# Banded attention and a token/channel mixer on one core: the next batch's attention interleaved with this batch's channel layer, scores by key chunk, gathers once

## The chip, the cores and the metric

The kernel runs on one core of a Trainium2 chip. The metric is the device time of one execution in microseconds (us); lower is better. The core has five engines that run side by side, each with its own queue in order: TensorE (PE, matmuls; its weight loads are listed as PEld), VectorE (DVE), ScalarE (ACT), GpSimd (POOL) and SyncE (SP, which here only issues DMAs). Matmul results land in PSUM (8 banks of 512 float32 columns on 128 partitions) and are read from there by DVE or ACT.

## The reference

```python
scores = scale * np.matmul(q, k.transpose(0, 1, 3, 2))     # q, k, v: (8, 8, 576, 64)
mask = np.abs(pos[:, None] - pos[None, :]) <= 32
mask = mask | is_global[:, None] | is_global[None, :]      # 8 global positions
attn = softmax(np.where(mask, scores, -1e9))
x = (attn @ v), heads side by side                         # (8, 576, 512)
h = np.maximum(x.T @ w_tok1, 0.0) @ w_tok2                 # 576 -> 256 -> 576, per channel
u = x + h.T
out = u + np.maximum(u @ w_ch1, 0.0) @ w_ch2               # 512 -> 1536 -> 512
```

Eight batches are computed one by one. The 576 positions make four tiles of 128 and a leftover of 64.

## The kernel before

One loop over the batches `b`; the code of a batch is written attention first, then the two mixer layers. A framework allots buffers from pools, sets the waits and orders each engine's queue; a later batch can run ahead only as far as that order and the buffers allow.

Attention, per head pair `hp`: ten transposes bring q and k to `qT`, `kT` (L244, copied out of PSUM by DVE at L250, L252). Four small matmuls (L258, L259) transpose the global rows, which eight one-row DMAs per tensor and batch have gathered (L223). Per head then: for each of five shifted key chunks `c` two or three score matmuls (L274, L277, L284) whose weights are the 64x128 half of `kT` that belongs to the head, `Exp` on ACT (L287), the band mask on DVE (L288); two matmuls of the global keys against all queries (L291, L292); five `og` matmuls for the global queries (L298); and for each query tile up to four matmuls of 65 columns (L310, L312, L313, L314), a reciprocal and a product on DVE (L316, L317) into `x16`.

Mixer: `pa1` (L326) and `ph_` (L339) are the token layer, `pu` (L352) transposes `u16` to `uT`. `pb1` (L362) is the first channel matrix: 24 groups of four matmuls of 288 columns, `Relu` on ACT (L369). `ph2` (L374) is the second: five groups of twelve matmuls of 512 columns, the last with 64 query rows only, then the addition of `u16` on DVE (L382) and the store, issued by ACT (L383).

Ahead of the loop stand masks, and the four weight matrices: loaded as float32 by SP and cast to float16 by ACT (L161 to L177). The first is loaded ahead of batch 0's q.

Of the kernel before, what the change touches and what calls it, by code (L numbers as in the profile page):

```python
# [9 lines left out]
F32 = mybir.dt.float32  # L11
F16 = mybir.dt.float16
I32 = mybir.dt.int32
AF = mybir.ActivationFunctionType
ALU = mybir.AluOpType


@with_exitstack
def kernel(
# [36 lines left out]
    nat = ctx.enter_context(tc.tile_pool(name="nat", bufs=3))
    ab = ctx.enter_context(tc.tile_pool(name="ab", bufs=2))
    hb = ctx.enter_context(tc.tile_pool(name="hb", bufs=2))
    pb = ctx.enter_context(tc.tile_pool(name="pb", bufs=3))
    mb = ctx.enter_context(tc.tile_pool(name="mb", bufs=2))  # L60
    ob = ctx.enter_context(tc.tile_pool(name="ob", bufs=2))
    tiny = ctx.enter_context(tc.tile_pool(name="tiny", bufs=3))
    psA = ctx.enter_context(tc.tile_pool(name="psA", bufs=5, space=bass.MemoryType.PSUM))
    psM = ctx.enter_context(tc.tile_pool(name="psM", bufs=3, space=bass.MemoryType.PSUM))

    def psa(shape, dtype=F32, name="pa"):
        return psA.tile(shape, dtype, tag="a", name=name)

    def psm(shape, dtype=F32, name="pm"):
# [17 lines left out]
    iota_i_i = const.tile([P, S], I32)
    nc.gpsimd.iota(iota_i_i, pattern=[[1, S]], base=0, channel_multiplier=0)
    iota_if = const.tile([P, S], F32)
    nc.vector.tensor_copy(out=iota_if, in_=iota_i_i)  # L90
    iota_p_i = const.tile([P, 1], I32)
    nc.gpsimd.iota(iota_p_i, pattern=[[1, 1]], base=0, channel_multiplier=1)
    iota_pf = const.tile([P, 1], F32)
    nc.vector.tensor_copy(out=iota_pf, in_=iota_p_i)

    colng = const.tile([P, S], F16)
    tmp_s = const.tile([P, S], F32, tag="set576")
    nc.vector.tensor_scalar(out=colng, in0=iota_if, scalar1=gidx_bf[:, 0:1], scalar2=None, op0=ALU.not_equal)
    for g in range(1, NG):
        nc.vector.tensor_scalar(out=tmp_s, in0=iota_if, scalar1=gidx_bf[:, g : g + 1], scalar2=None, op0=ALU.not_equal)  # L100
        nc.vector.tensor_mul(out=colng, in0=colng, in1=tmp_s)

    iota_tm_i = const.tile([P, NT, P], I32)
    nc.gpsimd.iota(iota_tm_i, pattern=[[P, NT], [1, P]], base=0, channel_multiplier=0)
    iota_tmf = const.tile([P, NT, P], F32)
    nc.vector.tensor_copy(out=iota_tmf, in_=iota_tm_i)
    selq = const.tile([P, NT, P], F16)
    nc.vector.tensor_scalar(
        out=selq[0:NG], in0=iota_tmf[0:NG], scalar1=gidx_pf[0:NG, 0:1], scalar2=None, op0=ALU.is_equal
    )  # L110
# [303 lines left out]
```

## Time and profile before

| | us |
|---|---|
| median of the timed runs | 717.95 (712.82, 717.95, 717.98) |
| profiled execution, first to last instruction | 716.0 |
| its PE busy / DVE / ACT / POOL | 613.9 / 315.9 / 298.4 / 6.4 |
| first `Exp` of batch 0 | 76.8 |
| from one batch's attention to the next's | about 80 |

The profile holds no time of its execution other than that span; the median of the timed runs lies 1.95 us above it. A matmul's row runs until its result has left the array, so rows of a stream overlap: the cost of one in a stream is the distance from start to start, not its duration. The granted clock is a share of TensorE's full speed.

### The profile page before, as it was taken

How to read it: one execution, taken by the hardware profiler on the slowest of the kernel's cores; microseconds unless marked ns; L12 is line 12 of the kernel's file. 1: busy time of each engine (PE TensorE's matmuls, PEld its weight loads, DVE VectorE, ACT ScalarE, POOL GpSimd, SP SyncE). 2: the span in 40 equal slices, each digit the busy share in tenths (PEclk: the TensorE clock that was granted, in tenths of full speed). 3: DMA queues.
4: the chain of work that ended last, by engine and by line, in shares of the span. 5: the costliest groups of instructions: out<-in, count | busy, mean ns of one | idle time of the engine just before them, and what ended most of it. 6: DMA issues, size and time to landing. Idle time of an engine off the chain costs nothing.

```text
span 716.0 us, 12722 instructions
## 1 busy us (share of the span) xinstructions
PE 613.9 (86%) x4576; PEld 366.7 (51%) x4576; DVE 315.9 (44%) x1441; ACT 298.4 (42%) x742; POOL 6.4 (1%) x27
## 2 busy tenths in 40 slices
PE   0001599999999999999999999999999999999997
PEld 0000365555646566555546565656556555656563
DVE  2800355326552456415551456326651565145521
ACT  1243364416525453346326533554337432523350
POOL 3000000000000000000000000000000000000000
PEclk9999999995559855796569855995579756975599
DMA  1992553026300907013600436020900100010001
GB/s 48 287 250 33 93 111 69 1 88 113 62 1 3 204 5 134 0 50 85 114 15 16 126 70 123 1 78 5 198 1 30 41 2 1 16 52 2 1 1 66
DMA packets 125054, 46.43 MB, mean 65 GB/s; under 512 B 117504, under 2 KB 118080, under 8 KB 124992
## 3 DMA queue, kind: packets, MB, share of 16 engines
q1 hardware_dynamic: 119744, 36.19, 25.5%
q10 hardware_dynamic: 5248, 9.44, 3.8%
q8 instruction: 35, 0.57, 0.4%
q14 instruction: 27, 0.22, 0.1%
HBM read 36.18 MB, written 9.44 MB: 64 GB/s over the span
## 4 chain that ended last, share of the span: by engine, by line
PE 74%; DVE 8%; DMA 6%; SPq 6%; ACT 3%; issue 2%; ACTq 0%; DVEq 0%
SPq L223 2%; DMA w_32_216<-in_moe_w_tok_dram 2%; DMA wc_32_226<-in_moe_w_ch_dram 2%; SPq L200 1%; SPq L192 1%; SPq L182 1%; ACT wc_228 L172 1%; DMA w_32_222<-in_moe_w_tok_dram 1%; DMA n_1_2_2532<-in_k_dram 1%; DMA out_dram<-osb_3_1373 0%; PE ph_5_0_6982 L374 0%; PE ph_7_4_9314 L374 0%; PE ph_3_4_4778 L374 0%; PE ph_2_4_3644 L374 0%; PE ph_1_4_2510 L374 0%
## 5 line engine op out<-in xcount | busy, mean ns | idle before, releaser
L362 PEld LDWEIGHTS <-wc_228 128*128 128x128 f16 x768 | 75.0, 98 | 19.6
L244 PE MATMUL pT_0_0_332<-ident,qn_277 128*128 128x128 f16 (+1 forms) x5 | 0.8, 292 | 40.3 <-ACT qn_277 L208 40.3
L314 PEld LDWEIGHTS <-selq 8*128 8x128 f16 (+1 forms) x320 | 27.7, 123 | 5.3 <-issue 3.1
L244 PEld LDWEIGHTS <-qn_277 128*128 128x128 f16 (+1 forms) x20 | 1.8, 125 | 41.5 <-ACT qn_277 L208 40.3
L326 PEld LDWEIGHTS <-w_219 128*128 128x128 f16 (+1 forms) x80 | 9.1, 123 | 24.6 <-issue 24.1
L244 PE MATMUL pT_0_1_339<-ident,kn_278 128*128 128x128 f16 (+1 forms) x5 | 0.8, 293 | 15.9 <-ACT kn_278 L208 15.9
L244 PEld LDWEIGHTS <-kn_278 128*128 128x128 f16 (+1 forms) x20 | 1.8, 126 | 17.0 <-ACT kn_278 L208 16.0
L339 PEld LDWEIGHTS <-w_224 128*128 128x128 f16 (+1 forms) x80 | 7.8, 114 | 5.2 <-issue 3.3
L172 ACT CAST wc_228<-wc_32_226 128x6144 f16<-128x6144 f32 x1 | 5.3, 5312 | 10.8 <-DMA wc_32_226<-in_moe_w_ch_dram 10.8
L258 PE MATMUL pG_0_346<-ident,qg_320 8*64 8x8 f16 x2 | 0.2, 210 | 11.2 <-DVE qg_320 L227 11.2
L374 PEld LDWEIGHTS <-b_5_6837 128*128 128x128 f16 (+1 forms) x60 | 5.9, 100 | 7.4 <-issue 0.8
L374 PEld LDWEIGHTS <-b_0_1167 128*128 128x128 f16 (+1 forms) x60 | 5.9, 100 | 7.0 <-issue 0.4
L374 PEld LDWEIGHTS <-b_1_2301 128*128 128x128 f16 (+1 forms) x60 | 5.9, 100 | 7.0 <-issue 0.4
L374 PEld LDWEIGHTS <-b_4_5703 128*128 128x128 f16 (+1 forms) x60 | 5.9, 100 | 7.0 <-issue 0.4
L374 PEld LDWEIGHTS <-b_3_4569 128*128 128x128 f16 (+1 forms) x60 | 5.9, 100 | 7.0 <-issue 0.4
L374 PEld LDWEIGHTS <-b_2_3435 128*128 128x128 f16 (+1 forms) x60 | 5.9, 100 | 7.0 <-issue 0.4
L374 PEld LDWEIGHTS <-b_7_9105 128*128 128x128 f16 (+1 forms) x60 | 5.9, 100 | 7.0 <-issue 0.4
L374 PEld LDWEIGHTS <-b_6_7971 128*128 128x128 f16 (+1 forms) x60 | 5.9, 100 | 7.0 <-issue 0.4
L177 ACT CAST wc_232<-wc_32_230 128x6144 f16<-128x6144 f32 x1 | 5.3, 5311 | 9.0 <-DMA wc_32_230<-in_moe_w_ch_dram 9.0
L252 DVE COPY kT_0_329<-pT_0_1_339 128x576 f16<-128x576 f16 x1 | 0.5, 458 | 16.2 <-PE pT_0_1_339 L244 16.2
L287 ACT ACTIVATE E_0_353<-sc_0_0_354 128x136 f16<-128x136 f32 x1 | 0.3, 284 | 15.9 <-PE sc_0_3_371 L284 15.9
L382 DVE TENSOR_TENSOR osb_0_9263<-u_7_9053,ph_7_0_9250 128x512 f32<-128x512 f16 x1 | 0.7, 687 | 14.1 <-PE ph_7_0_9250 L374 14.1
(5049 smaller groups left out, 1988.4 us busy)
## 6 DMA issues: line engine op xcount, KB each, us to landing
wc_32_226<-in_moe_w_ch_dram SPq DMA_DIRECT2D x1, 3072.0 KB
wc_32_230<-in_moe_w_ch_dram SPq DMA_DIRECT2D x1, 3072.0 KB
n_0_0_258<-in_q_dram SPq DMA_DIRECT2D x4, 256.0 KB
n_1_0_264<-in_k_dram SPq DMA_DIRECT2D x4, 256.0 KB
n_0_1_1392<-in_q_dram SPq DMA_DIRECT2D x4, 256.0 KB
n_1_1_1398<-in_k_dram SPq DMA_DIRECT2D x4, 256.0 KB
n_0_2_2526<-in_q_dram SPq DMA_DIRECT2D x4, 256.0 KB
n_1_2_2532<-in_k_dram SPq DMA_DIRECT2D x4, 256.0 KB
```

The source lines that it names most:

```text
L172: nc.scalar.copy(out=wc1, in_=wc1_32)
L177: nc.scalar.copy(out=wc2, in_=wc2_32)
L182: nc.sync.load(r, gidx_i[0:1, g : g + 1])
L192: nc.sync.dma_start(out=d32[0 : np_t[t], t], in_=ten[b, :, P * t : P * t + np_t[t], :].rearrange("h p d -> p h d"),)
L200: nc.sync.dma_start(out=d32[r0:r1, t], in_=ten[b, :, j0 : j0 + (r1 - r0), :].rearrange("h p d -> p h d"),)
L223: nc.sync.dma_start(out=d32[g : g + 1], in_=ten[b, :, ds(gregs[g], 1), :].rearrange("h one d -> one h d"))
L244: nc.tensor.transpose(out=pT[:, P * t : P * t + npt], in_=src[0:npt, t, 2 * hp : 2 * hp + 2, :], identity=ident[0:npt, 0:npt],)
L314: nc.tensor.matmul(ox[0:nq], lhsT=selq[0:NG, tau, 0:nq], rhs=ogs, start=False, stop=True)
L326: nc.tensor.matmul(pa1, lhsT=w1[0:npt, ch, P * tt : P * tt + P], rhs=x16[0:npt, ch, :], start=(ch == 0), stop=(ch == NT - 1),)
L339: nc.tensor.matmul(ph_[0:nq], lhsT=w2[:, ch, P * tau : P * tau + nq], rhs=a1[:, ch, :], start=(ch == 0), stop=(ch == 1),)
L362: nc.tensor.matmul(pb1, lhsT=wc1[:, cc, P * j : P * j + P], rhs=uT[:, cc, NSH * half : NSH * half + NSH], start=(cc == 0), stop=(cc == 3),)
L374: nc.tensor.matmul(ph2[0:nq], lhsT=b1[:, j, P * tau : P * tau + nq], rhs=wc2[:, j, :], start=(j == 0), stop=(j == 11),)
```

## The change

The program is written anew as functions: `T` (transposes of a head pair), `S_` (scores of a pair), `GK`, `OG`, `PV` (attention), `M1` to `M3` (token layer and transposes), `M4`, `M5` (channel layer). `sparse(b)` lists the first eight of batch `b`, `dense(b)` the channel layer, and `merge` writes `sparse(b + 1)` and `dense(b)` into each other by the costs given with each piece.

- Scores: queries lie as `[8 global | 128]` per tile, so that one matmul per head and key chunk gives the 64 nearest columns of the tile ahead, the global columns and the tile itself (200 or 136 columns); the two heads of a pair use rows 0-63 and 64-127 and fill one PSUM tile, which ACT reads in one instruction.
- Global keys of all eight heads come from eight matmuls (`GK`), global queries of all heads from ten (`OG`); `PV` takes both corrections as one more matmul of 264 columns per half, 18 matmuls a tile (10 for the last).
- The 64 leftover rows of an even batch and of the next odd one share one 128-row tile in `M4l` and `M5`.
- Global rows are gathered once, for all batches, by 16 indirect DMAs of POOL. The weights are loaded by POOL's queue with a cast to float16. POOL also casts v, copies global columns and clears borders.
- q, k and v have one float32 buffer each; the load for `b + 2` waits for the cast of `b + 1`.
- PSUM: two 2-bank tiles for `T`, `S_`, `GK`, `OG`, `M1`, `M2`; one for `PV`, `M3`; two 1-bank tiles for `M4`, `M5`. Before: 5 and 3 single banks.

```diff
+def merge(sparse, dense):
...
+        if j >= len(dense) or (i < len(sparse) and a / ts <= d / td):
+            a += sparse[i][0]
+            sparse[i][1]()
...
+        else:
+            d += dense[j][0]
+            dense[j][1]()
...
+    for b in range(B):
+        nc.gpsimd.indirect_dma_start(
+            out=v32g[b], out_offset=None, in_=rows[2],
...
+    nc.gpsimd.dma_start(out=w1, in_=moe_w_tok1[0 : S - LAST, :].rearrange("(c p) x -> p c x", p=P))
...
+        nc.scalar.copy(out=s["qn"][:, sl], in_=n32[0][:, sl])
+        nc.vector.tensor_copy(out=s["kn"][:, sl], in_=n32[1][:, sl])
+        nc.gpsimd.tensor_copy(out=vsh[b % 2][:, sl, :, 0:D], in_=n32[2][:, sl])
...
+            for par in range(2):
+                r = slice(64 * par, 64 * par + 64)
+                nc.tensor.matmul(
+                    ps[:, par, off : off + n], lhsT=kT[r, P * c : P * c + P], rhs=qf[r, lo : lo + n],
+                    start=True, stop=True,
+                )
...
+        nc.gpsimd.tensor_copy(
+            out=eg[:, :, 2 * p : 2 * p + 2, 0:NG], in_=e2[:, :, :, P:QS].rearrange("p h c x -> p c h x")
+        )
...
+        u += [(0.6, lambda p=p: T(b, p)) for p in range(2)]
+        u += [(0.5, lambda: S_(b, 0)), (0.6, lambda: T(b, 2)), (0.5, lambda: S_(b, 1)), (0.6, lambda: T(b, 3))]
+        u += [(0.5, lambda: S_(b, 2)), (0.5, lambda: S_(b, 3)), (0.4, lambda: GK(b)), (1.1, lambda: OG(b))]
+        u += [(0.8, lambda t=t: PV(b, t)) for t in range(NT)]
...
+        u = [(0.86, lambda j=j: M4(b, j)) for j in range(NJ)]
+        if b % 2:
+            u += [(0.9, lambda j=j: M4l(b, j)) for j in range(3)]
+        u += [(0.64, lambda t=t, i=i: M5(b, t, i)) for t in range(4 + b % 2) for i in range(4)]
...
+        if b + 2 < B:
+            load(b + 2)
+        merge(sparse(b + 1) if b + 1 < B else [], dense(b))
```

TensorE's queue where batch 2's first channel matrix ends, before:

```order
L362 MATMUL pb1_2_11_0_3568<-uT_2_3404,wc1_228 128x288
L362 LDWEIGHTS wc1_228
...
L362 MATMUL pb1_2_11_1_3574<-uT_2_3404,wc1_228 128x288
L374 LDWEIGHTS b1_2_3435
L374 MATMUL ph2_2_0_3580<-wc2_232,b1_2_3435 128x512
```

And in the change, where batch 2's `M4` (`b1p`) stands with batch 3's scores (`s1`, `s2`) and transposes (`pT`):

```order
L492 MATMUL b1p_2_3_1859<-uT_2_1716,wc1_274 128x512
L336 LDWEIGHTS kT_3_1_1806
L336 MATMUL s1_3_1_1865<-qT_3_1_1805,kT_3_1_1806 128x200
...
L492 MATMUL b1p_2_4_1884<-uT_2_1716,wc1_274 128x512
L336 LDWEIGHTS kT_3_1_1806
L336 MATMUL s2_3_1_1871<-qT_3_1_1805,kT_3_1_1806 128x136
...
L315 LDWEIGHTS qn_3_1747
L315 MATMUL pT_3_3_1890<-ident_108,qn_3_1747 128x128
```

Between two groups of the channel layer now stand a group of scores or ten transposes of the next batch.

ScalarE's queue at the same place, before (`b1` is the Relu of the channel layer, `a1` that of the token layer):

```order
L295 ACTIVATE Egk_2_7_3318<-gk2_2_7_3315 8x64
L333 ACTIVATE a1_2_3368<-pa1_2_0_3369 128x512
L333 ACTIVATE a1_2_3368<-pa1_2_1_3376 128x512
L369 ACTIVATE b1_2_3435<-pb1_2_0_0_3436 128x288
L369 ACTIVATE b1_2_3435<-pb1_2_0_1_3442 128x288
```

And in the change (`e_all` is `Exp` of the scores, `qn_5` the cast of batch 5's q):

```order
L345 ACTIVATE e_all_247<-s1_3_1_1865 128x2x2x200
L495 ACTIVATE b1_2_1787<-b1p_2_4_1884 128x512
L352 ACTIVATE e_all_247<-s2_3_1_1871 128x2x136
L353 ACTIVATE e_all_247<-s2_3_1_1871 128x2x136
L354 ACTIVATE e_all_247<-s2_3_1_1871 128x2x200
L293 CAST qn_5_2797<-n32_q_82 128x2560
L495 ACTIVATE b1_2_1787<-b1p_2_5_1907 128x512
L345 ACTIVATE e_all_247<-s1_3_2_1913 128x2x2x200
```

The Relus of the channel layer now stand between the `Exp`s of the next batch, and a whole cast ahead of one of them.

POOL's queue in the change at the end of batch 0's scores (`eg` holds the exponentials of the global queries, which `OG` reads; before, POOL has nothing after its masks):

```order
L320 COPY qT_2_0_1223<-gT_q_286 128x5x8
L302 COPY kgz0_251<-gT_k_287 64x4x8 x2
L320 COPY qT_2_1_1253<-gT_q_286 128x5x8
L295 CAST vsh1_256<-n32_v_84 128x40x64
L358 COPY eg_249<-e_all_247 128x5x2x8
L303 TENSOR_TENSOR vg0_253<-v32g_2_290,d2_160 128x8x64
L295 CAST vsh0_255<-n32_v_84 128x40x64
```

The last of batch 0's four `eg` copies stands behind the cast of batch 1's v (`vsh1`).

## Rows read from the trace of the kernel before

**Rows 1.** The page's first part: span, then busy time of each engine, share, instructions.

```profile
span 716.0 us, 12722 instructions
PE 613.9 (86%) x4576; PEld 366.7 (51%) x4576; DVE 315.9 (44%) x1441; ACT 298.4 (42%) x742; POOL 6.4 (1%) x27
```

**Rows 2.** Busy time by stretch, batch 1 (its length; engines; granted clock; DMA share, GB/s).

```profile
160.00:205.00 45.00, 41.76 (x357) 26.22 (x356) 25.87 (x144) 23.99 (x66) 0.00 (x0) 0.53 0.41 76
205.00:217.00 12.00, 11.72 (x57) 4.78 (x56) 6.93 (x21) 1.19 (x2) 0.00 (x0) 0.65 0.01 1
217.00:228.00 11.00, 11.00 (x91) 8.79 (x90) 1.00 (x3) 9.08 (x23) 0.00 (x0) 1.00 0.00 0
228.00:241.50 13.50, 13.50 (x66) 6.12 (x63) 3.08 (x5) 2.24 (x3) 0.00 (x0) 1.00 0.53 133
```

**Rows 3.** The chain of waits: start, us, what; matmuls of 512 columns.

```profile
205.73 0.85 PE pa_1_0_2235 L326 x2
228.42 2.59 PE ph_1_0_2446 L374 x12
709.47 2.72 PE ph_7_4_9314 L374 x12
```

**Rows 4.** Timeline of PE, transposes of 128 columns at full clock: start, us, what.

```profile
296.30 0.40 PE L352 MATMUL pu_0_3405<-ident,u_2_3383 128*128 128x128 f16 x4
296.53 0.39 PE L352 MATMUL pu_1_3411<-ident,u_2_3383 128*128 128x128 f16 x4
```

**Rows 5.** Timeline of PE, 65 columns: same tile shape, then a change of shape.

```profile
481.79 0.19 PE L310 MATMUL ox_0_0_6068<-vsh_5953,E_0_6023 128*128 128x65 f16 x1
481.82 0.19 PE L312 MATMUL ox_0_0_6068<-vsh_5953,E_0_6023 128*128 128x65 f16 x1
...
121.40 0.23 PE L313 MATMUL ox_7_2_1077<-vg_324,Egk_7_1050 8*128 8x65 f16 x1
121.57 0.24 PE L310 MATMUL ox_7_3_1085<-vsh_283,E_7_1016 128*128 128x65 f16 x1
```

**Rows 6.** Timeline of ACT: Exp of 136 and 264, Relu of 512, cast of 2048.

```profile
480.27 0.28 ACT L287 ACTIVATE E_0_6023<-sc_0_0_6024 128x136 f16<-128x136 f32 x1 [1.16 <-PE sc_0_0_6024 L284]
480.45 0.39 ACT L287 ACTIVATE E_0_6023<-sc_0_1_6029 128x264 f16<-128x264 f32 x1
...
126.00 0.60 ACT L333 ACTIVATE a_0_1100<-pa_0_0_1101 128x512 f16<-128x512 f32 x1 [5.46 <-PE pa_0_0_1101 L326]
...
249.24 1.88 ACT L208 CAST kn_3680<-n_1_3_3666 128x2048 f16<-128x2048 f32 x1
```

**Rows 7.** Timeline of DVE: copy of `qT`, five mask products, copy of `uT`, sum with PSUM.

```profile
252.29 0.46 DVE L250 COPY qT_1_2789<-pT_1_0_2793 128x576 f16<-128x576 f16 x1 [0.35 <-PE pT_1_0_2793 L244]
...
243.09 1.34 DVE L288 TENSOR_TENSOR E_0_2621<-E_0_2621,bandm 128x136 f16<-128x136 f16 x5 [0.81 <-ACT E_0_2621 L287]
...
297.01 0.41 DVE L355 COPY uT_3404<-pu_0_3405 128x512 f16<-128x512 f16 x1
...
480.10 0.68 DVE L382 TENSOR_TENSOR osb_4_5925<-u_4_5651,ph_4_4_5912 64x512 f32<-64x512 f16 x1 [2.02 <-DMA n_2_6_7074<-in_v_dram]
```

**Rows 8.** Timeline of the beginning: POOL, indices landed, one batch's q gathers, first Exp.

```profile
1.95 0.68 POOL L104 IOTA iota_tm_i<- 128x640 int32 x1
...
14.48 0.17 DVE L81 CAST gidx_bf<-gidx_b 128x8 f32<-128x8 int32 x1 [11.82 <-DMA gidx_b<-in_global_idx_dram]
...
54.69 12.46 SPq L223 DMA_DIRECT2D g_0_0_293<-in_q_dram  x8
...
76.78 0.28 ACT L287 ACTIVATE E_0_353<-sc_0_0_354 128x136 f16<-128x136 f32 x1 [15.92 <-PE sc_0_3_371 L284]
```

**Rows 9.** The page's third part: a DMA queue's packets, MB, share of 16 engines.

```profile
q1 hardware_dynamic: 119744, 36.19, 25.5%
```

More of the change, by code (lines that the diff above doesn't have):

```diff
@@ L15 @@
 ALU = mybir.AluOpType
+AX = mybir.AxisListType
+P = 128
+NT = 5
+NG = 8
+WIN = 32
+QS = P + NG
+EW = 2 * P + NG
+VW = 66
+def merge(sparse, dense):
+    ts, td = sum(c for c, _ in sparse) or 1.0, sum(c for c, _ in dense) or 1.0
+    i = j = 0
+    a = d = 0.0
+    while i < len(sparse) or j < len(dense):
+        if j >= len(dense) or (i < len(sparse) and a / ts <= d / td):
+            a += sparse[i][0]
+            sparse[i][1]()
+            i += 1
+        else:
+            d += dense[j][0]
+            dense[j][1]()
+            j += 1
 @with_exitstack
@@ L64 @@
[L64 to L69, printed above, removed]
-        return psM.tile(shape, dtype, tag="m", name=name)
+    ob = ctx.enter_context(tc.tile_pool(name="ob", bufs=3))
+    tiny = ctx.enter_context(tc.tile_pool(name="tiny", bufs=4))
+    psS = ctx.enter_context(tc.tile_pool(name="psS", bufs=2, space=bass.MemoryType.PSUM))
@@ L99 @@
[L99 to L110, printed above, removed]
@@ new lines, in GK @@
+    def GK(b):
+        s = st[b]
+        ps = pss([P, 2, 512], name=f"gk_{b}")
+        for p in range(NP):
+            o = ps[32 * p : 32 * p + 32]
+            qv = s["qT", p][:, :, NG:QS]
+            w = kgz[b % 2][:, p, :]
+            nc.tensor.matmul(o[:, 0, 0:384], lhsT=w, rhs=qv[:, 0:3], start=True, stop=True)
+            nc.tensor.matmul(o[:, 1, 0:256], lhsT=w, rhs=qv[:, 3:5], start=True, stop=True)
+        lf = mb.tile([P, NT * P], F16, tag="lf", name=f"lf_{b}")
+        nc.scalar.activation(out=lf[:, 0:384], in_=ps[:, 0, 0:384], func=AF.Exp, scale=scale)
+        nc.scalar.activation(out=lf[:, 384:640], in_=ps[:, 1, 0:256], func=AF.Exp, scale=scale)
+        nc.vector.tensor_mul(out=lf, in0=lf, in1=mf)
+        s["lf"] = lf
@@ new lines, in M1 @@
+    def M1(b):
+        s = st[b]
+        x16 = x16s[b % 2]
+        ps = pss([P, 2, 512], name=f"a1p_{b}")
+        for tt in range(2):
+            for ch in range(NT):
+                w = w1[:, ch, P * tt : P * tt + P] if ch < NT - 1 else w1l[:, b % 2, P * tt : P * tt + P]
+                nc.tensor.matmul(ps[:, tt, :], lhsT=w, rhs=x16[:, ch, :], start=(ch == 0), stop=(ch == NT - 1))
+        a1 = mb.tile([P, 2, DM], F16, tag="a1", bufs=1, name=f"a1_{b}")
+        nc.scalar.activation(out=a1, in_=ps, func=AF.Relu)
+        s["a1"] = a1
+        s["u16"] = mb.tile([P, 4, DM], F16, tag="u16", name=f"u16_{b}")
+        if b % 2 == 0:
+            s["ul"] = mb.tile([P, DM], F16, tag="ul", name=f"ul_{b}")
+        else:
+            s["ul"] = st[b - 1]["ul"]
@@ new lines, in dense @@
+    def dense(b):
+        u = [(0.86, lambda j=j: M4(b, j)) for j in range(NJ)]
+        if b % 2:
+            u += [(0.9, lambda j=j: M4l(b, j)) for j in range(3)]
+        u += [(0.64, lambda t=t, i=i: M5(b, t, i)) for t in range(4 + b % 2) for i in range(4)]
+        return u
+    for t in range(NT):
+        cast(0, t)
+    load(1)
+    gather_t(0)
+    gather_t(1)
+    globals_(0)
+    for _, f in sparse(0):
+        f()
+    for b in range(B):
+        if b + 1 < B:
+            cast(b + 1)
+            globals_(b + 1)
+        if b + 2 < B:
+            load(b + 2)
+        merge(sparse(b + 1) if b + 1 < B else [], dense(b))
```

644 lines of the change are left out of this document (355 added, 289 removed).

## The prediction

> **What bounds the kernel now.** I read the page's first part, then the busy times by stretch, then the chain of waits, then single rows of the timeline. The page says PE 86% busy [rows 1], which taken alone leaves 14% to win. The stretches say otherwise [rows 2]: the first row is one batch's attention, 45 us with a granted clock of 0.53, the other three its mixer, 36.5 us. In the attention PE counts 41.8 us as busy, but 357 merged rows of small matmuls at about half clock are not much work: by columns streamed (576 x 2 for transposes of each of four pairs, 1,232 of scores, 576 of global keys, 325 and 1,235 of outputs for each of eight heads) it is some 31,600, which at the rate below would take 13 us. The chain's rows give that rate [rows 3]: twelve matmuls of 512 columns take 2.59 us, 216 ns each or 0.42 ns a column, where the clock is 1.00; the token layer, which follows the attention, pays 0.85 us for two, 425 ns each, since the low clock lasts into it. So the kernel alternates between a stretch bound by short dependent steps at the lower level (1.2 GHz) and one bound by matmul columns at the higher (2.4 GHz), about 80 us a batch.
>
> **The change part by part.** All is summed in the profiled execution's own time, 716.0 us; the median of the runs is 1.95 us more, added at the end.
>
> *PE work of an iteration* (channel layer of `b`, attention and token layer of `b+1`), at full clock. `M4` and `M5`: 48 + 48 matmuls of 512 columns x 216 ns = 20.7 us. An odd `b` adds 48 matmuls of 128 columns and 12 of 512 for two batches' leftovers: transposes of 128 columns come 57 ns apart (four in 0.23 us, [rows 4]), so 48 x 57 ns + 12 x 216 ns = 5.3 us; before, each batch paid 12 x 0.216 us or more for its own leftover (the last of [rows 3]). Transposes: 40 + 16, x 57 ns = 3.2. Scores: 40 matmuls with 6,976 columns x 0.42 ns = 2.9. `GK` 2,560 columns, 1.1; `OG` 2,640, 1.1. `PV`: 10 x 264 columns, 1.1, and 72 of 66 columns; two of 65 columns with the same tile shape start 0.03 us apart [rows 5], so 2.2. `M1`, `M2`: 20 x 216 ns = 4.3. Sum 15.9 for the attention side, 36.6 us for an even iteration, 41.9 for an odd one.
>
> *Changes of tile shape.* From weights of 8 rows to weights of 128 the next matmul starts 0.17 us later [rows 5], where 65 columns at the low clock account for 0.05; I take 0.12 as the price of a change. Before, every head made several. Now eight score groups and `GK` are entered and left: 18 x 0.12 = 2.2 us. The trace has no row in which weights on rows 0-63 and on rows 64-127 alternate, as the 40 score matmuls now do. Nearest rows: no cost beyond columns, as between two of one shape, or a change each time, 40 x 0.12 = 4.8 us; below nothing by up to half of the 2.9 us, if the two halves overlap. I take no cost, since each half has its own rows and its own PSUM bank; range -1.5 to +4.8 us an iteration.
>
> The Trainium skill (TensorEngine Tiling (Array Packing), Key Properties under Tiling Modes) says that different tiles load and multiply in parallel. No run here shows it; by it the scores would cost 1.5 us instead of 2.9, and the whole 10 us less than my sum.
>
> *Waits in an iteration.* The other engines are not the bound. ACT: 0.28 us for 136 elements and 0.60 for 512 [rows 6] give 0.15 us + 0.88 ns an element: a pair's scores (800 + 272 + 272 + 400 elements) 2.1, x 4 = 8.5; `GK` 0.9; Relus 12 x 0.60 + 1.1 + 0.9 on average; a cast of 2,560 at the row's rate 2.4; together 21, and some 2 us for issuing stores. DVE: eight copies of 640 at the 576 row's rate, 4.1; eight mask products of 1,000 elements: five with 1,128 in all took 1.34, so about 0.7 each, 5.2; ten 512-column products and sums at 0.68 and two of twice that, 9.5; `uT` 1.6; the rest about 5 [rows 7]; together 25. POOL, idle before [rows 1], gets 2,560 elements of v at 1.06 ns (640 in 0.68 us, [rows 8]), 2.7, and some 3 of small copies. But PE, ACT and DVE each have one queue in order, and `T`, `S_` and the rest share two PSUM tiles. I went through TensorE's order of the even iteration `b = 2` with these prices and 0.1 to 0.2 us per handover. PE waits where a score group needs the tile of transposes that DVE copies only after two mask products (0.9 and 0.6 us); where `M4` 7 waits for a Relu behind the cast of q (0.8); where the last scores and `GK` wait for `Exp`s behind that cast (1.0 and 0.4); `M4` 8 the same way (0.8); `OG` for POOL's last copies (0.3): 4.8 us. From `PV` on, `M5`'s pieces of 0.65 to 1.3 us cover the 1.1 us of reciprocal and product between two tiles. Below this it can't fall much, while a late load or semaphore adds; I take 6.5. An iteration: 36.6 + 2.2 + 6.5 = 45.3 even, 41.9 + 2.2 + 6.5 = 50.6 odd. Iterations 0 to 6: 4 x 45.3 + 3 x 50.6 = 333 us.
>
> *The beginning.* It drops the ACT casts of weights and batch 0's gathers, which held its first `Exp` until 76.8 us [rows 8]. It gains a chain on POOL. The indices land 14.5 us into the program before; issued first and on ACT now, perhaps 13; some 20 tiny DVE steps later, at 18, POOL issues 16 gathers and 10 weight loads, then casts v and copies the columns that the first score needs. No row shows a DMA issued by POOL. Eight register-addressed ones cost SP 12.5 us, 1.6 each [rows 8]; a plain one can't cost less than nothing and SP's run near 0.5. 26 x 1.0 us (range 0.4 to 1.6) reach 44 us; v and globals another 5: first `Exp` near 50 (35 to 66). Then batch 0's attention is alone: scores 12 us by ACT and two tiles. Its last `eg` copy stands behind the cast of batch 1's v, which lands after 7 MB of weights and batch 1's q and k: 119,744 packets took 25.5% of 16 engines for 716 us [rows 9], so 24 ns each, 13,824 packets a batch, 21 us of all engines. I put that landing near 66, so `OG` starts at 70. `OG` and its product 2.5, five `PV` without cover 1.9 each, `M1` to `M3` 6: first iteration at 88 us (72 to 105).
>
> *The end.* Iteration 7 has no partner: 20.7 + 5.3 = 26 us and, from the last matmul's end (709.47 + 2.72) to the end of the span, 3.8 as before [rows 3]: 30.
>
> *Loads.* 21 us of the DMA engines' time per iteration of 45 to 50; the buffers are single, but the load for `b + 2` has a whole iteration from its cast to the next. No cost taken; if the cast of q comes before its data, each us stops ACT and PE.
>
> Sum: 88 + 333 + 30 = 451, less 3 for scores that overlap now and then, plus 2 for what lies outside the span: **450 us**.
>
> **The rivals.**
>
> *The clock falls in the scores.* Dense groups and small ones alternate there with short waits; before, the clock fell to 0.53 in the attention, which is small matmuls with gaps, and stood at 1.00 in `pb1`, an unbroken stream [rows 2]. The new stretch mixes the two. If it ran at the lower level, its 12 us of matmuls would take 24, of which 4 fill waits: 7 x 8 = 56 more, **506 us**.
>
> The Trainium skill (TensorE: Matmul & The Clock Gate, A second HAM failure mode) describes a kernel whose short idles between PSUM-cycled groups made the clock swing. Rows 2 show both levels, but no such alternation; by that rule it would be this rival.
>
> *The clock never rises: slower than before.* All matmuls at 425 ns per 512 columns: 36.6 and 41.9 become 72 and 82.5; with 2.2 and 3 us of waits 77 and 88, so 572 for seven iterations, 95 for the beginning, 56 for the end: **725 us**. It decides from a mean of 81 us an iteration. Against it: then PE would have no idle at all, and an unbroken stream is what ran at 1.00 in the third of [rows 2].
>
> *The queues in order hold more than I saw.* Waits of 13 us an iteration and the first iteration at 100: **508 us**. For it: three queues with casts in their midst, POOL's speed only guessed. Against: 20 us of slack on ACT and DVE.
>
> *Little waits.* Overlapping score halves, 3 us of waits, cheap POOL issues: 4 x 40 + 3 x 45 + 75 + 30 + 2 = **402 us**.
>
> *It does not interleave.* Excluded: the order shows dense groups between scores in TensorE's queue.
>
> **How the numbers follow.** Forecast 0.68, with its own range of 420 to 490; clock low in the scores 0.12; queues 0.10; little waits 0.08; clock never up 0.02. A range of **405 to 515** keeps the middle of both 500s and most of the low case. A measurement of this kernel tells about 1% from no change; every case but one is far faster: faster 0.97, same 0.01, slower 0.02.
>
> **What would show it.** Granted clock above 0.9 from the first iteration on, and distances of 45 and 51 us between the first `M4` groups of successive batches, alternating; wider even ones with a full clock mean waits, with a low clock the first rival. First `Exp` near 50 us, behind POOL; `OG` of batch 0 released by POOL after the cast of v. ACT near 190 us busy in all, DVE near 220, POOL 60. 2.59 us still for twelve `M5` matmuls undisturbed. The prediction is wrong if PE's idle time in an iteration is over 10 us, or if alternating halves of the array cost a change each.

## The result and the profile after

The median is 425.21 us (424.02 to 426.31) against 717.42: 0.594 of the time before, 95% interval 0.592 to 0.596. The forecast was 450 with a range of 405 to 515. The profiled execution spans 422.7 us. The page's first part and two rows of its second (40 slices of the span, in tenths), against [rows 1]:

```profile
span 422.7 us, 6930 instructions
PE 331.2 (78%) x2756; PEld 179.0 (42%) x2756; DVE 212.5 (50%) x434; ACT 150.0 (35%) x273; POOL 94.2 (22%) x197
PE   0120242678799979997999799979998999899995
DMA  1999999996927094616660847100110021001012
```

PE is busy for a smaller share than before, yet the time fell by two fifths: its 613.9 us were 4,576 matmuls, those of the attention at about half the clock [rows 2], and now there are 2,756. The first nine slices are the beginning, the others are nearly full. The same kernel by stretch, cut at the first `M4` of each batch (columns as in [rows 2]): batch 0's attention from its first `Exp` on, iterations 0, 1, 2, 5 and 6, and the end.

```profile
50.36:94.69 44.33, 22.85 (x217) 14.24 (x213) 22.14 (x36) 11.55 (x21) 12.16 (x26) 1.00 1.11 202
94.69:137.68 42.99, 38.95 (x302) 20.02 (x302) 21.83 (x38) 17.41 (x32) 8.04 (x16) 0.92 0.63 133
137.68:183.06 45.38, 42.21 (x376) 23.33 (x373) 23.92 (x43) 19.13 (x35) 7.85 (x16) 1.00 0.51 108
183.06:223.49 40.43, 37.02 (x320) 19.86 (x318) 23.43 (x41) 17.45 (x32) 7.60 (x16) 1.00 0.55 115
...
309.33:353.10 43.77, 42.43 (x376) 23.33 (x373) 22.48 (x42) 17.05 (x34) 1.73 (x8) 1.00 0.08 31
353.10:391.48 38.38, 36.65 (x310) 19.17 (x307) 21.71 (x40) 15.26 (x31) 1.12 (x4) 1.00 0.09 28
391.48:422.68 31.20, 26.20 (x160) 13.13 (x156) 4.22 (x7) 8.96 (x15) 0.00 (x0) 1.00 0.15 51
```

So the sum is 94.7 for the beginning (88 forecast), 296.8 for iterations 0 to 6 (333), 31.2 for the end (30). Iterations 5 and 6 differ from 1 and 2 in that no cast of q, k or v is left: 1.6 and 2.0 us less (in iteration 6, some 0.6 of it because ten transposes fewer fall into it).

The clock column of the first row is not to be believed. In the timeline of PE, `PV` matmuls of 66 columns, same tile shape, at 75 and at 82.6 us (as [rows 5]):

```profile
75.10 0.26 PE L412 MATMUL pv_0_543<-vsh_255,e_all 128*128 128x66 f16 x1
75.17 0.25 PE L417 MATMUL pv_0_543<-vsh_255,e_all 128*128 128x66 f16 x1
75.23 0.25 PE L412 MATMUL pv_0_543<-vsh_255,e_all 128*128 128x66 f16 x1
...
82.61 0.19 PE L412 MATMUL pv_3_609<-vsh_255,e_all 128*128 128x66 f16 x1
82.64 0.20 PE L417 MATMUL pv_3_609<-vsh_255,e_all 128*128 128x66 f16 x1
82.68 0.19 PE L412 MATMUL pv_3_609<-vsh_255,e_all 128*128 128x66 f16 x1
```

Their starts stand 0.06 us apart at first and 0.03 later: batch 0's attention ran at the lower level until about 82 us.

The beginning in the timeline, several engines (against [rows 8]): first `Exp`, the cast of batch 1's v, the last `eg` copy behind it, and `OG`.

```profile
50.36 0.84 ACT L345 ACTIVATE e_all<-s_0_0_405 128x800 f16<-128x800 f32 x1 [10.66 <-PE s_0_0_405 L336]
68.58 2.32 POOL L295 CAST vsh_256<-n_v 128x2560 f16<-128x2560 f32 x1 [5.93 <-DMA n_v<-in_v_dram]
70.84 0.25 POOL L358 COPY eg<-e_all 128x80 f16<-128x80 f16 x1
71.15 2.38 PE L382 MATMUL og_528<-vsh_255,eg 128*128 128x264 f16 x10 [10.88 <-POOL eg L358]
```

What PE waits for in iteration 2 and then in iteration 5 (the view of waits: who, for what, us):

```profile
PE b1p_8_1991 L492 <- ACT b_2_1787 L495: 1.0, 1, 1.0
PE og_1976 L382 <- POOL eg L358: 0.6, 1, 0.6
PE b1p_7_1970 L492 <- ACT b_2_1787 L495: 0.6, 1, 0.6
PE s_3_3_1938 L336 <- ACT e_all L354: 0.4, 1, 0.4
PE gk_1957 L369 <- ACT e_all L345: 0.3, 1, 0.3
PE s_3_1_1871 L336 <- DVE kT_2_1854 L323: 0.3, 1, 0.3
PE s_3_2_1919 L336 <- DVE kT_3_1902 L323: 0.2, 1, 0.2
...
PE b1p_11_3551 L492 <- ACT b_5_3329 L495: 0.8, 1, 0.8
PE s_6_1_3419 L336 <- DVE kT_2_3402 L323: 0.3, 1, 0.3
```

The seven waits of iteration 2 are those that the prediction had named, with the same releasers; they come to 3.4 us where 4.8 had been counted. In iterations 1 to 4, PE stands idle for 3.2 to 3.4 us each.

### The profile page after: what moved, and what is told of

Same layout as the page of the kernel before. It is cut to its first block, busy times and chain, and to the rows that moved or that the text cites. A ratio compares the mean times of both kernels' runs of the same rounds, so it can differ in the third digit from the quotient of the medians.

```text
span 422.7 us, 6930 instructions
## 1 busy us (share of the span) xinstructions
PE 331.2 (78%) x2756; PEld 179.0 (42%) x2756; DVE 212.5 (50%) x434; ACT 150.0 (35%) x273; POOL 94.2 (22%) x197
## 4 chain that ended last, share of the span: by engine, by line
PE 58%; ACT 11%; DVE 11%; DMA 9%; POOL 5%; issue 4%; POOLq 0%; DVEq 0%; ACTq 0%
ACT e_all L345 4%; DVE e_all L357 3%; DMA gidx_b<-in_global_idx_dram 3%; DMA n_v<-in_v_dram 3%; ACT e_all L354 2%; ACT e_all L353 2%; DMA w_271<-in_moe_w_tok_dram 1%; DMA g_k_281<-in_k_dram,idx_i 1%; ACT e_all L352 1%; POOL eg L358 1%; DVE x_0_257 L424 1%; POOL vsh_255 L295 1%; DMA n_k<-in_k_dram 1%; PE op_4_4516 L518 1%; PE op_4_3805 L518 1%
## 5 line engine op out<-in xcount | busy, mean ns | idle before, releaser
L357 DVE TENSOR_TENSOR e_all<-e_all,bandm 128x1000 f16<-128x1000 f16 x64 | 40.8, 678 | 53.3 <-ACT e_all L354 49.9
L492 PEld LDWEIGHTS <-wc_274 128*128 128x128 f16 x384 | 34.4, 98 | 45.4 <-issue 16.2
L358 POOL COPY eg<-e_all 128x80 f16<-128x80 f16 x32 | 10.5, 327 | 81.7 <-DVE e_all L357 80.9
L412 PEld LDWEIGHTS <-e_all 128*128 128x128 f16 x320 | 24.9, 100 | 3.0 <-issue 1.7
L417 PEld LDWEIGHTS <-e_all 128*128 128x128 f16 x256 | 19.1, 101 | 1.3
L382 PEld LDWEIGHTS <-eg 128*128 128x128 f16 x80 | 8.1, 109 | 21.3 <-POOL eg L358 19.5
L295 POOL CAST vsh_256<-n_v 128x2560 f16<-128x2560 f32 x4 | 9.3, 2316 | 29.9 <-PE pv_4_1063 L412 8.6
L295 POOL CAST vsh_255<-n_v 128x512 f16<-128x512 f32 (+1 forms) x8 | 9.8, 1263 | 24.4 <-DMA n_v<-in_v_dram 9.3
L315 PE MATMUL pT_0_371<-ident,qn_322 128*128 128x128 f16 x5 | 1.4, 289 | 16.9 <-ACT qn_322 L293 16.9
L454 PEld LDWEIGHTS <-w_273 128*128 128x128 f16 x80 | 7.8, 97 | 12.0 <-issue 3.2
L505 PEld LDWEIGHTS <-wc_274 128*128 128x128 f16 x192 | 11.1, 98 | 0.9
L315 PEld LDWEIGHTS <-qn_322 128*128 128x128 f16 x20 | 1.9, 127 | 18.7 <-ACT qn_322 L293 17.7
L436 PEld LDWEIGHTS <-w_271 128*128 128x128 f16 x64 | 6.3, 99 | 7.3 <-issue 1.1
L293 ACT CAST qn_697<-n_q 128x2560 f16<-128x2560 f32 x1 | 2.3, 2324 | 18.9 <-DMA n_q<-in_q_dram 18.9
L293 ACT CAST qn_322<-n_q 128x512 f16<-128x512 f32 x5 | 3.1, 617 | 12.7 <-DMA n_q<-in_q_dram 12.7
L315 PE MATMUL pT_0_371<-ident,kn_323 128*128 128x128 f16 x5 | 1.4, 288 | 7.4 <-DVE kn_323 L294 7.4
L518 PEld LDWEIGHTS <-b_7_4324 128*128 128x128 f16 x48 | 4.7, 98 | 5.4
L293 ACT CAST qn_1189<-n_q 128x2560 f16<-128x2560 f32 x1 | 2.3, 2325 | 12.8 <-DMA n_q<-in_q_dram 12.8
```

The lines of the kernel that those rows point to most:

```text
L295: nc.gpsimd.tensor_copy(out=vsh[b % 2][:, sl, :, 0:D], in_=n32[2][:, sl])
L357: nc.vector.tensor_mul(out=eh, in0=eh, in1=bandm)
L358: nc.gpsimd.tensor_copy(out=eg[:, :, 2 * p : 2 * p + 2, 0:NG], in_=e2[:, :, :, P:QS].rearrange("p h c x -> p c h x"))
L382: nc.tensor.matmul(ps[:, hf, 0 : 4 * VW], lhsT=eg[:, c], rhs=vsh[b % 2][:, c, 4 * hf : 4 * hf + 4, :], start=(c == 0), stop=(c == NT - 1),)
L412: nc.tensor.matmul(o, lhsT=e_all[:, h, tau, QS - sh : QS - sh + P], rhs=vsh[b % 2][:, tau, h, :], start=False, stop=last and tau == NT - 1,)
L417: nc.tensor.matmul(o, lhsT=e_all[:, h, tau + 1, 0:P], rhs=vsh[b % 2][:, tau + 1, h, :], start=False, stop=last)
```

## The experiments

Theory: the gain is made by the interleaving, which hides the small steps' waits and keeps the clock up, and by a cheaper attention; what an iteration still loses stands in the queues of ACT, DVE and POOL, and so does the beginning. Rivals: the rewritten attention alone makes the gain; the beginning is bound by its transfers. All runs change the new kernel. Ratios are to the kernel before, with 95% intervals; for the new kernel 0.594 (0.592 to 0.596).

| | median us | ratio | span | first `Exp` | first `M4` | iterations 0, 1, 2, 5, 6 |
|---|---|---|---|---|---|---|
| the change | 425.2 | 0.594 | 422.7 | 50.4 | 94.7 | 43.0, 45.4, 40.4, 43.8, 38.4 |
| e1 in sequence | 545.9 | 0.763 (0.760 to 0.766) | 544.2 | 50.6 | 95.7 | 57.2, 62.6, 57.2, 62.0, 57.1 |
| e2 halves grouped | 427.2 | 0.599 (0.596 to 0.601) | 423.2 | 50.3 | 95.3 | 42.9, 45.4, 40.4, 43.8, 38.4 |
| e11 one half only | 427.0 | 0.598 (0.595 to 0.600) | 426.1 | 50.5 | 95.0 | 44.0, 45.6, 40.7, 44.3, 38.9 |
| e3 q cast by POOL | 418.7 | 0.587 (0.584 to 0.590) | 416.5 | 50.7 | 93.9 | 39.0, 45.2, 40.0, 43.8, 38.4 |
| e8 q cast late | 412.9 | 0.579 (0.576 to 0.582) | 410.6 | 50.5 | 94.2 | 37.7, 43.8, 38.9, 43.8, 38.4 |
| e7 leftovers alone | 441.3 | 0.619 (0.616 to 0.622) | 438.2 | 50.6 | 94.6 | 44.8, 46.3, 44.8, 44.4, 42.3 |
| e4 weights late | 418.9 | 0.587 (0.584 to 0.589) | 416.8 | 39.2 | 92.7 | 38.0, 45.4, 40.4, 43.8, 38.4 |
| e5 gathers split | 414.0 | 0.580 (0.578 to 0.583) | 412.6 | 39.8 | 89.6 | 38.0, 45.4, 40.4, 43.8, 38.4 |
| e6 v of batch 0 on ACT | 411.0 | 0.576 (0.573 to 0.579) | 410.0 | 47.4 | 85.9 | 39.1, 45.4, 40.4, 43.8, 38.4 |
| e9 eg copy first | 416.6 | 0.583 (0.579 to 0.588) | 415.0 | 50.8 | 86.8 | 43.1, 45.4, 40.4, 43.8, 38.4 |
| e10 together | 396.1 | 0.553 (0.551 to 0.556) | 395.9 | 39.2 | 79.5 | 38.0, 43.8, 38.8, 43.8, 38.4 |

**e1, no interleaving.**

```diff
-        merge(sparse(b + 1) if b + 1 < B else [], dense(b))
+        merge([], dense(b))
+        merge(sparse(b + 1) if b + 1 < B else [], [])
```

> The channel layer of a batch and the attention of the next are written one after the other; everything else stays. Theory A (the interleaving is what pays, by covering the waits of the small steps and by keeping the clock up): batch 0's attention and token layer, which run alone in the change, took 34 us of the 44 between its first Exp and the first M4 when the wait for the v of batch 1 is taken off; with a channel layer of 21 or 26 us behind it that is 55 to 60 us a batch instead of 42.5, so 7 x 13 to 7 x 17 more: 515 to 545 us, with the granted clock falling in every attention. Theory B (the rewritten attention itself is what pays): 35.2 and 40.5 us of matmuls at full clock plus some 10 us of waits, 47 to 50 us a batch: 460 to 480 us with the clock up. Not worth more than 2% either way: the interleaving doesn't matter.

545.9 us, 0.9 above the upper end of theory A's range and far from theory B's: theory A. By stretch: batch 1's channel layer, the next attention, and within that a part that the records show at the lower level:

```profile
152.90:180.00 27.10, 27.10 (x176) 13.90 (x173) 4.31 (x8) 9.92 (x18) 0.12 (x1) 1.00 0.11 40
180.00:215.50 35.50, 21.19 (x202) 13.16 (x201) 19.23 (x35) 9.97 (x19) 7.29 (x15) 0.71 0.60 108
183.70:204.20 20.50, 11.69 (x111) 7.53 (x109) 9.81 (x18) 6.02 (x11) 4.60 (x12) 0.50 0.67 116
```

Of the 293 us between before (716.0) and the change (422.7), the interleaving makes 121 and the rewritten attention, beginning and leftovers 172, taken in this order; the old attention interleaved was not run. From iteration 1 on a batch takes 17 to 19 us longer in sequence: PE stands idle for 14 to 15 us instead of 1 to 3, and the other 5 to 6 us are work at the lower level, which lasts 17 to 20.5 us in each attention. The rewritten attention alone doesn't keep the clock; with dense groups between its steps it does.

**e2 and e11, the two halves of the rows.** e2 groups the score matmuls by head, e11 puts both on the same half.

```diff
-        score(s1, 0, 1)
-        score(s1, 200, 2)
+        for par in range(2):
+            score(s1, 0, 1, [par])
+            score(s1, 200, 2, [par])
...
```

> In each score tile the matmuls of the head on rows 0-63 come first, then those of the head on rows 64-127, instead of taking turns. Theory A (matmuls on different halves of the rows run at the same time): a pair's columns on the path go from 872 (200+200+136+136+200) to 600 + 808 = 1,408, so four pairs cost 0.9 us more; the 40 score matmuls of iterations 5 and 6, 2.16 us in the change, take about 3.0, and the run 5 to 7 us more (430 to 432). Theory B (they run one after the other whatever the order, 6,976 columns or 2.9 us, and the 2.16 us has another cause): no change in either. Theory C (each alternation costs a change of tile shape): grouped ones are cheaper, below 2.16 us, and the run 2 to 5 us less.

```diff
-                r = slice(64 * par, 64 * par + 64)
+                r = slice(0, 64)
```

> The changed kernel, but both score matmuls of a pair use rows 0-63, so the odd heads' scores are computed from the even heads' q and k (the odd heads' own scores are left out); number, size and order of all matmuls stay. Theory A (the halves run at the same time, so that the third in the queue overtakes the second in e2): a pair's 1,744 columns now stand one behind the other, 0.73 us instead of the 0.33 us from its first to its last start in iterations 5 and 6, so the 40 score matmuls take 3.7 us instead of 2.16, and the run 8 to 13 us more, 433 to 438 us. Theory B (they are short because of something else, the weight loads or the pipelining): 2.16 us and 425 us as before.

By its numbers e2 is theory B: 2.2 us for the 40 matmuls, and no change that is clear of the noise (the intervals of e2 and the change meet at 0.596). But theory B's reason, one after the other, does not fit. The timeline of PE in e2, a pair's ten scores and the next `M4`:

```profile
313.06 0.57 PE L336 MATMUL s<-qT,kT 64*128 64x200 f16 x10
313.57 0.39 PE L494 MATMUL b1p<-uT,wc 128*128 128x512 f16 x1
```

0.51 us for 1,744 columns, which at 0.42 ns would take 0.73 one behind the other. The trace's single starts explain it: the first four are at 313.063, 313.070, 313.159, 313.166, that is, pairs 7 ns apart, although the program as built has the first half's two ahead of the second half's two. The next six stand in it as 136, 136, 200 columns for one half and then the same for the other; in the trace they start as 136, 136, 136, 136, 200, 200. Matmuls of the second half overtook those of the first (so TensorE does not start everything in the order of its queue, as the first section has it), and the order in the program didn't matter. e11 is the control. Six scores with the next work, in the change and then in e11:

```profile
320.54 0.38 PE L336 MATMUL s_6_2_3467<-qT_2_3401,kT_2_3402 64*128 64x136 f16 x6
320.76 0.34 PE L336 MATMUL s_6_3_3486<-qT_3_3449,kT_3_3450 64*128 64x200 f16 x4
```

```profile
319.51 0.58 PE L336 MATMUL s<-qT,kT 64*128 64x136 f16 x6
320.02 0.45 PE L315 MATMUL pT<-ident,qn 128*128 128x128 f16 x5
```

0.22 us became 0.51 (of which 0.09 is the change to another shape); from each group's first start to the next work the 40 took 3.62 us instead of 2.16 in iterations 5 and 6. So the halves do run at the same time: theory A of e11 by its mechanism, but not by its price. The median is 1.8 us more (the intervals of the two overlap) and the span 3.4, not 8 to 13, since an iteration's waits shrank by most of what the scores grew. PE's idle time in iteration 2 fell from 3.4 us (40.43 less 37.02 above) to 2.4:

```profile
184.60:225.28 40.68, 38.30 (x319) 21.30 (x317) 23.43 (x41) 17.50 (x32) 7.42 (x16) 1.00 0.56 114
```

**e3 and e8, the cast of q.**

```diff
-        nc.scalar.copy(out=s["qn"][:, sl], in_=n32[0][:, sl])
+        if b == 0:
+            nc.scalar.copy(out=s["qn"][:, sl], in_=n32[0][:, sl])
+        else:
+            nc.gpsimd.tensor_copy(out=s["qn"][:, sl], in_=n32[0][:, sl])
```

> The cast of q is done by POOL instead of ACT for batches 1 to 7. Theory A (the cast in the middle of ACT's queue is what PE waits for in iterations 0 to 4; 5 and 6 have none and take 1.6 to 2.0 us less): iterations 1 to 4 come to 43.8 and 38.4 us, iteration 0 loses its stretch at the low clock: 10 to 12 us less, 413 to 416 us. Theory B (the wait moves to POOL: eg copies and the column copies stand behind 2.3 us more of casts, OG waits): no gain, 422 to 430 us. ACT's Relus and Exps should then follow each other without a gap of 2.3 us in either.

```diff
-        nc.scalar.copy(out=s["qn"][:, sl], in_=n32[0][:, sl])
+        with tc.issue_after(st[b - 2]["gk"]) if b > 2 else ExitStack():
+            nc.scalar.copy(out=s["qn"][:, sl], in_=n32[0][:, sl])
...
```

> The cast of q stays on ACT, but stands behind the last Exp of the scores instead of in their midst. Theory A (the cast among the Exps costs each of iterations 1 to 4 1.6 to 2.0 us and iteration 0 the 6.8 us at the low clock): iterations 1 to 4 come to 43.8 and 38.5 us, iteration 0 to 39, the run 10 to 12 us less, 413 to 416 us. Theory B (as with POOL in e3, another wait takes its place): iterations 1 to 4 within 0.6 us of the change's 45.4 and 40.4, the run 418 to 425 us.

e8 is theory A, to the decimal in the iterations: 43.8 and 38.9 us; the run, 412.9 us, is just below its range. e3 lies between its two theories (418.7): of the 6.2 us by which its span is shorter, 4.0 come from iteration 0, which kept its clock; in iterations 1 to 4, 0.2 to 0.5 us shorter, another wait took the place of the old one. Its timeline, POOL and DVE, and then the same two mask products in the change:

```profile
141.51 2.32 POOL L296 CAST qn<-n_q 128x2560 f16<-128x2560 f32 x1 [0.26 <-PE pT L318]
142.28 2.67 DVE L360 TENSOR_TENSOR e_all<-e_all,bandm 128x1000 f16<-128x1000 f16 x2
145.41 0.55 PE L339 MATMUL s<-qT,kT 64*128 64x136 f16 x10 [1.36 <-DVE kT L326]
```

```profile
147.17 1.27 DVE L357 TENSOR_TENSOR e_all<-e_all,bandm 128x1000 f16<-128x1000 f16 x2
```

Beside POOL's cast the two products took 2.67 us instead of 1.27, the copy of `kT` came after them, and the next scores waited 1.36 us. From the products' start to the end of the cast (143.83) are 1.55 us: as if they had stood still for that time. The Trainium skill (SBUF — State Buffer, "SBUF: two separate sides") says that DVE with two inputs and GpSimd share a pair of ports as an exclusive lock, and the loser "fully blocks"; the trace agrees with its 1.4 us.

**e7, leftovers not paired** (`M4l` and the last `M5` for every batch, with 64 rows).

```diff
-        if b % 2:
-            u += [(0.9, lambda j=j: M4l(b, j)) for j in range(3)]
-        u += [(0.64, lambda t=t, i=i: M5(b, t, i)) for t in range(4 + b % 2) for i in range(4)]
+        u += [(0.9, lambda j=j: M4l(b, j)) for j in range(3)]
+        u += [(0.64, lambda t=t, i=i: M5(b, t, i)) for t in range(5) for i in range(4)]
...
```

> The changed kernel, but each batch does its 64 leftover rows by itself instead of two batches sharing a tile of 128. Theory A (an iteration is bound by TensorE's columns): an even batch gains 48 matmuls of 64 columns, 30 ns each, 12 of 512, 216 ns, and transposes, 4.2 us; an odd one loses 48 x 27 ns = 1.3 us: 4 x 4.2 - 4 x 1.3 = 12 us more, 435 to 439 us. Theory B (the added matmuls fill the 3.3 us of waits that an iteration has): 2 to 6 us more, 427 to 431 us.

15.5 us more in the profile, and 441.3 us, 2.3 above theory A's range: iterations 2, 4 and 6 take 3.9 to 4.4 more, about as worked out, odd ones not less but 0.6 to 0.9 more, the last batch 1.2 less. Theory A by its mechanism: here added columns show nearly one for one, unlike in e11; most of them come behind the scores, where the change's trace has no waits. In iteration 1 the 48 smaller `M4l` matmuls do take 0.9 us less, though they start 37 ns apart and not 30:

```profile
161.17 1.26 PE L503 MATMUL b1lp<-uTl,wc 128*128 128x64 f16 x30
```

But ten transposes of the next batch now stand ahead of its end (0.7 us more), and the leftover's own transposes come with a wait of 0.5. So part of what an even iteration costs is counted in the odd one before it.

**e4, e5, e6, e9 and e10, the beginning.** e4 writes the weight loads and the v gathers of later batches behind the first score steps; e5 lets POOL issue the gathers of batches 2 to 7 only after the last `eg` copy. The order of the beginning in e5:

```diff
+    first = [f for _, f in sparse(0)]
+    for f in first[:6]:
+        f()
+    weights()
+    for f in first[6:]:
+        f()
+    with tc.issue_after(st[0]["eg"].ins):
+        gather_v(range(2, B))
...
```

> POOL issues the weight loads and the v gathers of batches 1 to 7 after the small steps that batch 0's first scores need, and casts batch 0's v ahead of most of them. Theory A (the beginning is bound by POOL's queue): gathers from 15.8 us on, 9 x 1.25, casts of v 2.9, a few issues and copies: first Exp near 37 us instead of 50.4, v of batch 1 loads from 36 us on, the last eg copy no longer waits for its cast, OG near 49 instead of 71, first M4 near 73 instead of 94.7, the run 20 us less, 403 to 407 us. Theory B (the beginning is bound by the DMA engines, which are busy from 10 to 95 us): first Exp earlier, but the weights land later and the first M4 stays above 85, the run 415 to 425 us.

> As e4, but the v gathers of batches 2 to 7 stand behind batch 0's last eg copy in POOL's queue, and that of batch 1 ahead of the weight loads. Theory A (in e4 POOL stood still from 45 to 58 us because each further gather had to wait until an earlier weight load had landed, with the eg copies behind): first Exp one gather later, 40.5 us, OG near 53 instead of 68.1, first M4 near 77 instead of 92.7, the run 14 to 16 us less than e4: 402 to 406 us. Theory B (the loads set the time): OG near 53, but the token layer or the first transposes of batch 1 wait for their data; first M4 above 85, the run 411 us or more.

First `Exp` went to 39 us as POOL's queue had it, but `OG` only to 68.1 (e4) and 61.8 (e5). POOL in e4, then DVE and POOL in e5:

```profile
53.90 0.96 POOL L260 DMA_INDIRECT v32g<-in_v_dram,idx_i  x1 [2.39 <-DMA wc<-in_moe_w_ch_dram]
57.38 0.95 POOL L260 DMA_INDIRECT v32g<-in_v_dram,idx_i  x1 [2.53 <-DMA wc<-in_moe_w_ch_dram]
```

```profile
58.53 1.49 DVE L299 CAST kn<-n_k 128x2560 f16<-128x2560 f32 x1 [6.92 <-issue]
59.94 1.26 DVE L362 TENSOR_TENSOR e_all<-e_all,bandm 128x1000 f16<-128x1000 f16 x2
61.34 0.38 POOL L363 COPY eg<-e_all 128x80 f16<-128x80 f16 x1 [8.09 <-DVE e_all L362]
```

In e4 each of the last four gathers stood 1.3 to 2.5 us until an older weight load had landed, then a copy behind them 4.5 us until a gather had, and the `eg` copies with them. In e5 that is gone, and the copy waits for DVE's mask product, ahead of which DVE stood 6.9 us at the cast of batch 1's k, whose last part landed at 58.5. By total and first `M4` both runs lie where theory B put them (418.9 and 414.0 us, 92.7 and 89.6). But a transfer sets the time here only where something that waits for it stands ahead of batch 0's steps in a queue; e10 takes that away.

```diff
-        nc.gpsimd.tensor_copy(out=vsh[b % 2][:, sl, :, 0:D], in_=n32[2][:, sl])
+        if b == 0:
+            nc.scalar.copy(out=vsh[b % 2][:, sl, :, 0:D], in_=n32[2][:, sl])
+        else:
+            nc.gpsimd.tensor_copy(out=vsh[b % 2][:, sl, :, 0:D], in_=n32[2][:, sl])
```

> The changed kernel, with batch 0's v cast by ACT, which stands idle from 18 to 37 us, instead of by POOL at 45 us. Theory A (that cast holds the single v buffer, so v of batch 1 starts to load only at 48 us, lands at 68.6, and its cast stands ahead of the eg copy that OG needs): v of batch 1 lands near 50 us, OG starts at 59 to 61 us instead of 71.2, first M4 near 84, first Exp 2.9 us earlier, the run 10 to 12 us less, 413 to 416 us. Theory B (v of batch 1 lands late because the weights take the DMA engines): OG stays within 4 us of 71, the run at 421 us or more.

The size was about right (`OG` at 60.1 us; 411.0 us for 413 to 416, since iteration 0 also kept its clock), the reason half wrong. SP's issues of batch 1's v, in the change and then in e6:

```profile
45.87 16.11 SPq L103 DMA_DIRECT2D n_v<-in_v_dram  x5
```

```profile
39.35 19.27 SPq L103 DMA_DIRECT2D n_v<-in_v_dram  x5
67.97 2.32 POOL L298 CAST vsh<-n_v 128x2560 f16<-128x2560 f32 x1 [7.95 <-DMA n_v<-in_v_dram]
```

They began 6.5 us earlier, and the cast behind them starts at 68.0 instead of 68.6 (67.9 in e10, where they also begin early): the DMA engines, busy without a break in the page's row until then, set that landing. What helped is that the last `eg` copy now happened to stand ahead of that cast. e9 tests this by itself:

```diff
+        with tc.issue_after(st[0]["eg"].ins) if b == 1 else ExitStack():
-        nc.gpsimd.tensor_copy(out=vsh[b % 2][:, sl, :, 0:D], in_=n32[2][:, sl])
+            nc.gpsimd.tensor_copy(out=vsh[b % 2][:, sl, :, 0:D], in_=n32[2][:, sl])
...
```

> The changed kernel with two instructions of POOL exchanged: batch 0's last eg copy stands ahead of the cast of batch 1's v instead of behind it. Theory A (OG waited for nothing but that copy's place in the queue): OG starts at 61 to 62 us instead of 71.2, everything up to the first M4 comes 9 to 10 us earlier, 85, the run 9 to 10 us less, or 12 to 14 if iteration 0 then also keeps the clock: 411 to 416 us. Theory B (the late landing of batch 1's data decides, not the queue): the first M4 comes less than 4 us earlier and a wait for batch 1's rows stands ahead of it, the run 421 us or more.

`OG` at 63.3, first `M4` 7.9 us earlier: theory A, a little short. e10 takes all of it, with the casts of batch 1 behind batch 0's steps on each engine:

> All that helped, in one: the v gathers and weight loads as in e5, batch 0's v cast by ACT, the late cast of q of e8, and the casts of batch 1's q, k and v behind batch 0's steps on ACT, DVE and POOL. Theory A (each delay was a place in a queue): first Exp near 38 us, OG near 50, first M4 near 74, then 38, 43.8, 38.9, 43.8, 38.8, 43.8, 38.4 and 31.2 as in e8: 391 in the profile, 392 to 396 us. Theory B (with the queues clear the DMA engines bound the beginning, which are busy without a break from 12 us on): OG near 50, but PE waits for batch 1's rows or for the weights, first M4 at 80 or later: 398 us or more.

396.1 us, the fastest kernel here; its iterations are e8's. First `M4` is at 79.5, not 74: first `Exp` came 1 us later than worked out, `OG` at 52.7, and from there to `M4` 26.7 us, with PE at the lower level up to 73 us. Of PE's waits between first `Exp` and `M4` none is for a transfer, so theory A by its mechanism, at the upper end of its range.

## Why the prediction was right, and where its sum was off

**Right.** The mechanism: e1 shows that the clock and the covered waits come from the interleaving. Iterations alternate by 5.0 us (45.4 and 40.4; 5.3 was worked out), twelve `M5` and four `M4` matmuls kept their 216 ns, first `Exp` came at 50.4 (50), `OG` at 71.2 (70) and behind the cast of v by POOL, as e9 shows. The end took 31.2 (30). A little luck is in the 50: POOL's 26 issues took 29.4 us, from 15.8 on, where 26 from 18 on had been put in. One reading was wrong without effect: the scores before had 1,128 columns a head, as [rows 7] says, and not 1,232, and the 13 us worked out from them stay. 425 lies near the lower end of the forecast's own range of 420 to 490, because the iterations were put too high by 36 us; the beginning, put too low by 7, hid part of that.

**Off: the iterations, 296.8 for 333, two terms of about the same size.** First, scores, `GK` and the changes of shape: 2.9 + 1.1 + 2.2 = 6.2 us an iteration were put in as columns one behind the other. The trace has 2.16 for the scores with what leaving a group costs, 0.40 for `GK` (its four strips of 32 columns start within 0.02 us) and 0.1 for each of the seven groups entered (a first score starts 0.31 us after a 512-column matmul, not 0.22): about 3.2. The lower end, "-1.5 us", took the overlap for the scores alone, and the Trainium skill's rule (TensorEngine Tiling (Array Packing), Key Properties), that different tiles execute in parallel, was set aside as unseen; e2 and e11 agree with it. All other PE terms were 32.6 and measured 32.8. Second, the waits: 6.5 were put in, 4.8 counted and the rest for late loads. In iteration 2, 40.4 less 36.0 of work leaves 4.4, and no load was late. e11 shows that the two terms aren't independent: with the halves one after the other the waits shrink.

**Off: the beginning, 94.7 for 88.** From `OG` to `M4` 18 us were put in, and 23.5 measured. About half of the miss is the clock, since the prices were those of the full one: `OG` and its product took 3.8 for 2.5, and of five `PV`, put at 1.9 us each, the first three stand 2.5 apart (74.93, 77.44, 79.96, 82.49) and the next, past the rise, 1.9. The other half is `M1` to `M3`, 8.6 us for 6 at the full clock, where DVE's copies and sums come one after the other. The chain's last pieces, with the copies of batch 1's first `qT` and `kT` ahead of the second half of `uT`:

```profile
92.64 0.60 DVE uT_676 L475
93.24 0.40 DVE qT_0_731 L322
93.64 0.40 DVE kT_0_732 L323
94.03 0.61 DVE uT_676 L475
```

**The rivals.** *The clock falls in the scores* came true for some 7 us only, in iteration 0 (granted clock 0.92 above), after PE's waits of 0.4 to 1.0 us between 104 and 109 us. In e3, e6 and e8, where PE's idle time in iteration 0 is 1.3 to 2.6 us instead of 4.0, it stays up; but it also does in e7 with 3.6, and in e4 it falls for 3.4 us in iteration 4 instead. The four executions of e9 range from 415.1 us at a mean clock of 1.00 to 420.6 at 0.98. So what exactly brings the fall on stays open. *Queues hold more* was wrong in size, but what is left to win stood in those queues: by span, e8's 12 us and e10's 27. *Little waits* (402) had the iterations right, and the forecast did not: its 4 x 40 + 3 x 45 = 295 us, with overlapping halves and 3 us of waits, stand against 296.8 in the trace. Its beginning, 75, was wrong (94.7), and so the result lies halfway between 402 and 450. The clock never stayed down, so no run came near 725. Of the busy times foretold, DVE's was right (212 for 220); ACT's was put too high (150 for 190), POOL's too low (94 for 60), and neither engine bounds an iteration.

## What to carry to other kernels

When a stage of small dependent steps and a stage of dense matmuls alternate, interleaving them pays twice, for the covered waits and for the clock; its worth is measured by writing the same pieces in sequence. Behind it, look in every engine's queue for a long instruction for a later batch (a cast, a gather) that stands ahead of a short one that TensorE is waiting for: exchanging two instructions was worth 8 us, moving the cast of q 12. A cost that is put in for work next to a wait can't simply be added, since the wait shrinks with it (e11).

## What was not expected of the hardware

- A matmul on the other half of the rows overtook those ahead of it in the program (starts 7 to 10 ns apart in e2, 59 to 97 ns on one half in e11).
- A DMA issued by POOL occupied it 0.75 us for a load of 512 KB and 1.25 us for most gathers, from start to start; in e4 gathers issued behind large loads waited 1.3 to 2.5 us more for one of them to land.
- A mask product of DVE beside a cast by POOL: 2.67 us for two instead of 1.27 (e3).
